# Layernorm, window attention and a gated feed-forward block: three independent reorderings of a scheduled kernel (first projections and fetch, late weight casts, a chain of weight scales)

## The chip, the cores and the metric

One core of one Trainium2 chip runs the whole kernel. The metric is device time in microseconds of one execution, the median over runs. The engines are TensorE (PE, with its weight loads as PEld), VectorE (DVE), ScalarE (ACT), GpSimd (POOL) and SyncE (SP), which issues the DMAs.

## What is computed

```
xn = layernorm(x)                                  # x: 2048 x 512
q, k, v = split(xn @ wqkv)                         # 32 heads of 16
p  = softmax(q k^T / 4, causal, window of 256)
s  = (p v) @ wo                                    # 2048 x 512
h  = silu(xn @ w1) * (xn @ w3)                     # 2048 x 1792
out = x + s * silu(h @ w2)
```

Inputs and output are float32; the products are taken in halves of f16 (a high and a low part, three products for each), so that float32 accuracy is kept.

## The kernel before

**Tiles.** The 2048 tokens go in four tiles of 512, the 32 heads in four groups of eight, the 1792 hidden units in 14 blocks of 128 (w13 for a block of w1 and w3, w2 for the way back). Within a tile the kernel projects q, k (`project`) and v (`value`), sends q and k through DRAM (`dQ`, `dK`) to bring them back in the layout of the scores (`fetch`, tiles qa and KA), finds row maxima in a first pass over the scores (`pass1`, L665 on PE and L679 on DVE), and takes the scores again, masks them (L753 on DVE), exponentiates (L756 on ACT) and multiplies by v (L774 on PE). Gate and up products (L1036, with the silu at L1051 on ACT, L1055 and L1060 on DVE), and the product with w2 (L1261) fill PE between attention steps.

**Weights.** In the first tile each weight block is loaded, its squares summed (L249 and L923 on ACT, `squares`), the sums cast (`sb`, L261 or L927 on DVE), summed over partitions on PE by a product with ones (L280 or L285), and turned into a power of two by a few one-column instructions on DVE (`powers`, L291 to L304). The block is then scaled and cut in two f16 parts: by `split` (L333 on ACT, L334 on DVE), or by `split_pool` (scale L342 and high part L343 on ACT, low part L345 on POOL). For w13, `measure` does this; for w2, `measure_down`, whose chain L935 to L945 joins the w2 norms with the power of the blocks before.

**Order.** PE runs in the order that the code gives. For the other engines a scheduler places the instructions by priority and data, within bounds set by hand: `later(n, f)` calls f n steps ahead, a step being one call of the main list; `besides` and `beside_scores` run a read beside the next bank of scores; `tc.issue_after(x)` forbids an instruction to be placed ahead of x on its engine; `lasts["emptied"]` is the last instruction that emptied a PSUM bank, and `lasts["exp"]` the last exponential (`behind_exp`). `high_priority` sections (`urgent`) come first.

**PSUM.** There are two banks m (`bank`), two banks of scores s (`scores_bank`) and the banks po. A bank is filled by PE and read by DVE or ACT; PE waits when the bank that comes next isn't read. A projection's bank is emptied by L614 (ACT, high part) and L618 (DVE, low part), one of gate and up by L1051 and L1055 or L1060.

**Start.** While the first weights arrive PE runs idle products with ones (`keep_busy`, L1537) to stay busy; behind them the transposes of the first tokens (L493), then the first projections `k00` and `q00`.

Of the kernel before, what the change touches and what calls it, by code (L numbers as in the profile page):

```python
# [10 lines left out]
F32 = mybir.dt.float32  # L11
# [10 lines left out]
P = 128  # L22
S = 2048
D = 512
F = 1792
H = 32
DH = 16
# [56 lines left out]
def tile_block(ctx: ExitStack, tc: tile.TileContext, x, wqkv, wo, w1, w3, w2, out):  # L84
# [155 lines left out]
    def squares(parts, on_act=0, apart=0):  # L240


        ssq = small.tile([P, len(parts)], F32, name="ssq")

        def one(i, raw):

            sq = ppool.tile([P, D], BF16, name="sqa" if i < on_act else "junk", bufs=1)
            if i < on_act:
                nc.scalar.activation(sq, raw, AF.Square, accum_out=ssq[:, i:i + 1])  # L249
            else:  # L250
                nc.vector.tensor_tensor_reduce(out=sq, in0=raw, in1=raw, scale=1.0, scalar=0.0,
                                               op0=ALU.mult, op1=ALU.add, accum_out=ssq[:, i:i + 1])
        for i, raw in enumerate(parts):
            if apart:
                later(apart * (i + 1), lambda i=i, raw=raw: one(i, raw))
            else:
                one(i, raw)
        sb = small.tile([P, len(parts)], BF16, name="sb")

        def cast():  # L260
            lasts["cast"] = nc.vector.tensor_copy(sb, ssq)  # L261
        def behind_bank():

            with tc.issue_after(lasts["emptied"].ins) if "emptied" in lasts else nullcontext():
                cast()
        if apart:
            later(apart * (len(parts) + 1) + 1, behind_bank)
        else:
            cast()
        return sb  # L270
# [310 lines left out]
    def project(t, g, k, terms=(range(3),), scores_bank=False):  # L581


        cell = {}

        parts = ([[(c, i) for c in (2 * half, 2 * half + 1) for i in range(3)] for half in range(2)] if len(terms) == 1
                 else [[(c, i) for i in group for c in range(NC)] for group in terms])

        def part(n):
            assert turned[t] == 4  # L590
            w = WQ[t, g, k]
            xh, xl = X[t]
            if n == 0:
                cell["pp"] = pss.tile([P, 2, TW], F32, name="s")[:, 0, :] if scores_bank else bank([P, TW])
            for c, i in parts[n]:
                a, b = ((0, xh), (1, xh), (0, xl))[i]
                nc.tensor.matmul(cell["pp"], w[:, (a * NC + c) * P:(a * NC + c + 1) * P], b[:, c, :], start=(c, i) == parts[0][0],  # L597
                                 stop=(c, i) == parts[-1][-1])
            if n < len(parts) - 1:
                return  # L600
            if t == 0:
                def store():
                    with behind_load():
                        nc.sync.dma_start(dWQ[g, k], w)
                    give(w, after=8)
                later(45, store)
            else:
                give(w)
            pp = cell["pp"]
            both = take(F16)  # L610
            B = both.rearrange("p (a t) -> p a t", a=2)
            s = QS / (XS * WS)
            with urgent():
                nc.scalar.activation(B[:, 0, :], pp, AF.Copy, scale=s)  # L614

            def rest():
                with urgent():
                    lasts["emptied"] = nc.vector.scalar_tensor_tensor(B[:, 1, :], pp, s, B[:, 0, :], op0=ALU.mult, op1=ALU.subtract)  # L618
                d = (dQ, dK)[k][g][:, :, t * TW:(t + 1) * TW]
                if k == 0:  # L620
                    nc.sync.dma_start(d[:, 0:2, :], B[:, 0:1, :].to_broadcast([P, 2, TW]))
                    nc.sync.dma_start(d[:, 2, :], B[:, 1, :])
                else:
                    nc.sync.dma_start(d[:, 0:2, :], B)
                    nc.sync.dma_start(d[:, 2, :], B[:, 0, :])
                give(both, after=4)
            later(1, rest)
        return opening([(len(l), lambda n=n: part(n)) for n, l in enumerate(parts)])
# [2 lines left out]
        WQ[t, g, k] = w = take(F16)  # L631
        nc.sync.dma_start(w, dWQ[g, k])

    def fetch(t, g):
        QA[t, g] = qa = qpool.tile([P, 4, TW], F16, name="qa")
        ka = keys(t, g)
        c0 = 0 if t else 2 * P
        for dst, d in ((ka[:, :, c0:], dK[g][:, :, t * TW - 2 * P + c0:(t + 1) * TW]),
                       (qa, dQ[g][:, :, t * TW:(t + 1) * TW])):
            for r in range(2):  # L640
                lasts["load"] = nc.sync.dma_start(dst[64 * r:64 * r + KR],
                                  d[64 * r:64 * r + 64].rearrange("(a d) i t -> (d i) a t", d=DH))

# [224 lines left out]

    measured = set()

    def measure(f, apart=0):

        raws = [RAW.pop(f + i) for i in range(2)]
        sb = squares([raws[0][0], raws[1][0], raws[0][1], raws[1][1]], on_act=4 if f > 2 else 2, apart=apart)
# [7 lines left out]
        def rest(pp, pi):  # L884
# [5 lines left out]
            def cut(i, k):  # L890
                if k == 0:
                    WF[0, f + i] = [[None, None], WF.pop((0, f + i), [None, None])[1]]
                WF[0, f + i][0][k] = a = take(F16)
                split_pool(a[:, 0:D], a[:, D:], raws[i][k], pi[:, k, i:i + 1])
                give(raws[i][k], after=5)
            for i in range(2):
                for k in range(2):
                    later(((1, 2, 4, 6) if f < 8 else (1, 5, 9, 13))[2 * i + k], lambda i=i, k=k: cut(i, k))
        if started:
            beside_scores(8, scale)  # L900
        else:
            later(10 if apart else 6, scale)

# [11 lines left out]
    def measure_down(k, f):  # L915
# [12 lines left out]

        def scale(s):
            p2 = small.tile([P, n], F32, name="pp2")  # L930
            return then(s, powers(sb, n, p2, None, s), lambda: rest(p2))

        def rest(p2):
            assert measured >= set(range(f0, f1))
# [12 lines left out]
            def cut(f):  # L947
# [3 lines left out]
                    with tc.issue_after(lasts["emptied"].ins):  # L951
                        split(b[:, 0:D], b[:, D:], raw, sw[:, f - f0:f - f0 + 1])
                else:
                    split_pool(b[:, 0:D], b[:, D:], raw, sw[:, f - f0:f - f0 + 1])
                give(raw, after=5)
            for i, f in enumerate(range(f0, f1)):
                later(1 + 2 * i, lambda f=f: cut(f))
# [335 lines left out]
    def total(t, b):  # L1293
# [4 lines left out]
        def part(half):  # L1298
# [16 lines left out]
            if half:  # L1315
# [10 lines left out]
                if t == NT - 1:  # L1326
                    store()
                else:
                    later(4, store)
                if b == 3:  # L1330
                    give(*(OT[t, g] for g in range(NG)))
        return opening([(6, lambda h=h: part(h)) for h in range(2)])
# [22 lines left out]
    def feed_forward():  # L1355
# [4 lines left out]
        for t in range(NT):  # L1360
            for f in range(FB):
                if t == 0:
# [3 lines left out]
                    elif f + LEAD == FB - 1:  # L1366
                        pieces += [(0, lambda f=f: load(0, f)) for f in range(FB - 2, FB)]
                    if f % 2 and f + 3 < FB:
                        pieces.append((0, lambda f=f + 3: later(5, lambda: measure(f, 1)) if f == 6 else measure(f, 1)))
                    pieces += [(0, lambda f=f: load_down(0, f)) for f in range(f + 2 if f else 0, min(f + 3, FB))]  # L1370
                    for m in range(f + 1 if f else 0, min(f + 2, FB)):
                        k = next(k for k, (_, f1) in enumerate(GROUPS) if m < f1)
# [158 lines left out]
        nc.gpsimd.memset(KA[2][:, a, :].bitcast(F32), TWO_ONES)  # L1531


    def keep_busy(n):
        ps = bank([P, 4, P])
        for _ in range(n):
            nc.tensor.matmul(ps, onesb, onesb.unsqueeze(1).to_broadcast([P, 4, P]), start=True, stop=True)  # L1537

# [19 lines left out]
        flush()  # L1558
    with tc.issue_after(lasts["hi"].ins), tc.issue_after(lasts["x"].ins):
        qk[1][1]()  # L1560
    keep_busy(4)


    k00, q00 = (project(0, 0, k, ((0,), (1,), (2,)), k) for k in (1, 0))
    run([k00[0], q00[0], k00[1]])
    qk[1][2]()
    with tc.issue_after(lasts["scale"].ins):
# [2 lines left out]
    qk[1][3]()  # L1570
    with tc.issue_after(lasts["hi"].ins):
        run([k00[2], q00[2]])
    later(1, lambda: fetch(0, 0))
    k01 = project(0, 1, 1, ((0, 2), (1,)))
    run(k01[:1])
    wv[2]()
# [4 lines left out]
    sc["o"] = scaled(SQ["wv"][3], OS / WS, "so")  # L1581
    with tc.issue_after(lasts["hi"].ins):
        measure(0)
    run(project(0, 1, 0, scores_bank=True))
    later(1, lambda: fetch(0, 1))
    run(value(0, True))
    qk[2][1]()
# [89 lines left out]
```

## Time and profile before

| | |
|---|---|
| median of 3 runs | 811.51 us (811.10 to 811.94) |
| the profiled execution, whole | 811.24 us |
| its span | 809.4 us |
| granted PE clock | 1.0 |
| PE busy | 793.7 us, 98% |
| DVE busy | 631.2 us, 78% |
| ACT busy | 392.1 us, 48% |
| POOL busy | 377.1 us, 47% |
| DMA moved | 134.19 MB, mean 166 GB/s |

A row of a timeline has the start in microseconds, the duration (of xN instructions of one form together), engine, line, operation and tiles, and in brackets the engine's idle time ahead of it with the instruction that ended it. A row of the table of waits has the sum, the number of times, and the longest.

### The profile page before, as it was taken

How to read it: one execution, taken by the hardware profiler on the slowest of the kernel's cores; microseconds unless marked ns; L12 is line 12 of the kernel's file. 1: busy time of each engine (PE TensorE's matmuls, PEld its weight loads, DVE VectorE, ACT ScalarE, POOL GpSimd, SP SyncE). 2: the span in 40 equal slices, each digit the busy share in tenths (PEclk: the TensorE clock that was granted, in tenths of full speed). 3: DMA queues.
4: the chain of work that ended last, by engine and by line, in shares of the span. 5: the costliest groups of instructions: out<-in, count | busy, mean ns of one | idle time of the engine just before them, and what ended most of it. 6: DMA issues, size and time to landing. Idle time of an engine off the chain costs nothing.

```text
span 809.4 us, 23944 instructions
## 1 busy us (share of the span) xinstructions
PE 793.7 (98%) x9176; PEld 403.7 (50%) x9176; DVE 631.2 (78%) x2037; ACT 392.1 (48%) x591; POOL 377.1 (47%) x732
## 2 busy tenths in 40 slices
PE   8999989999999999999999999999999999999998
PEld 4444444444444444444444454456544754466465
DVE  8788788887888777887988888777778787875437
ACT  6879586553546544345344433344444234344411
POOL 2345376342329445354353455530346276550670
PEclk9999999999999999999999999999999999999999
DMA  9968554835576474757655634646372644335321
GB/s 282 265 214 267 160 183 134 278 114 191 160 199 208 134 232 139 218 142 263 160 162 181 194 104 119 185 137 179 105 201 74 160 139 137 113 90 172 111 65 62
DMA packets 109795, 134.19 MB, mean 166 GB/s; under 512 B 18864, under 2 KB 64880, under 8 KB 109680
## 3 DMA queue, kind: packets, MB, share of 16 engines
q1 hardware_dynamic: 109392, 132.13, 54.6%
q8 instruction: 72, 1.18, 0.6%
q10 hardware_dynamic: 288, 0.52, 0.2%
q14 instruction: 43, 0.35, 0.1%
HBM read 91.23 MB, written 36.57 MB: 158 GB/s over the span
## 4 chain that ended last, share of the span: by engine, by line
PE 79%; DVE 8%; ACT 6%; DMA 3%; issue 2%; SPq 1%; POOL 0%; ACTq 0%; DVEq 0%
PE m L1036 30%; PE po L774 8%; PE m L1261 8%; PE m L1179 8%; PE m L597 7%; PE s L746 5%; PE m L1313 4%; PE m L567 4%; PE s L665 3%; DMA slot<-in_B_w_dram 2%; DVE junk L679 2%; PE po L665 2%; ACT slot L342 1%; ACT pt L756 1%; ACT sqa L249 1%
## 5 line engine op out<-in xcount | busy, mean ns | idle before, releaser
L1036 PE MATMUL m<-XH,slot 128*128 128x512 f16 x896 | 267.4, 380 | 1.6 <-DVE slot L618 1.2
L756 ACT ACTIVATE pt<-s,es 128x1024 f32<-128x1024 f32 x152 | 167.5, 1112 | 193.7 <-DVE s L753 186.5
L1036 PEld LDWEIGHTS <-slot 128*128 128x128 f16 x1344 | 124.7, 98 | 156.0 <-issue 12.0
L1036 PE MATMUL m<-XL,slot 128*128 128x512 f16 x448 | 169.9, 379 | 0.0
L753 DVE TENSOR_TENSOR s<-s,MK 128x256 f32<-128x256 f32 (+2 forms) x280 | 118.7, 434 | 51.2 <-PE s L746 47.0
L679 DVE CUSTOM_DVE_ANT_0 junk<-s,MW 128x320 bf16<-128x320 f32 x276 | 133.9, 485 | 17.9 <-PE s L665 10.3
L339 POOL TENSOR_TENSOR slot<-slot,slot 128x256 f16<-128x256 f32 (+1 forms) x86 | 57.7, 692 | 141.9 <-ACT slot L1069 76.7
L345 POOL TENSOR_TENSOR slot<-slot,slot 128x128 f16<-128x128 f32 x168 | 69.1, 446 | 58.3 <-ACT slot L343 58.3
L679 DVE CUSTOM_DVE_ANT_0 junk<-po,MW 128x320 bf16<-128x320 f32 x172 | 83.4, 485 | 4.7 <-DVE mt L704 0.3
L1261 PE MATMUL m<-slot,slot 128*128 128x512 f16 x336 | 78.6, 380 | 0.3 <-DVE slot L1055 0.3
L774 PE MATMUL po<-pt,V 64*32 64x320 f32 (+4 forms) x2880 | 77.2, 342 | 0.8 <-DVE pp L304 0.8
L597 PE MATMUL m<-XH,slot 128*128 128x512 f16 x240 | 71.0, 380 | 1.6 <-DVE slot L1055 1.2
L1179 PE MATMUL m<-slot,slot 128*128 128x256 f16 x588 | 68.4, 273 | 0.0
L1094 POOL TENSOR_TENSOR slot<-slot,slot 128x256 f16<-128x256 f32 x98 | 64.6, 671 | 1.1
L1051 ACT ACTIVATE slot<-m,sgs 128x512 f32<-128x512 f32 x56 | 38.3, 683 | 54.4 <-PE m L1036 52.3
L774 PEld LDWEIGHTS po<-pt,V 64*32 64x32 f32 x2880 | 50.5, 106 | 22.9 <-PE s L515 0.9
L1179 PEld LDWEIGHTS <-slot 128*128 128x128 f16 x588 | 56.1, 98 | 11.5 <-issue 3.0
L1055 DVE SCALAR_TENSOR_TENSOR slot<-slot,m 128x512 f32<-128x512 f32 x56 | 38.3, 684 | 29.0 <-ACT slot L1051 29.0
L746 PE MATMUL s<-qa,KA 50*64 50x320 f16 (+3 forms) x1472 | 58.4, 260 | 0.1
L597 PEld LDWEIGHTS <-slot 128*128 128x128 f16 x384 | 35.6, 98 | 44.8 <-issue 3.4
L746 PEld LDWEIGHTS <-KA 50*64 50x64 f16 x1472 | 30.1, 106 | 51.9 <-issue 30.9
L1261 PEld LDWEIGHTS <-slot 128*128 128x128 f16 x336 | 30.7, 98 | 38.6 <-issue 4.2
(189 smaller groups left out, 1138.5 us busy)
## 6 DMA issues: line engine op xcount, KB each, us to landing
slot<-dW SPq DMA_DIRECT2D x98, 256.0 KB
slot<-in_B_w_dram SPq DMA_DIRECT2D x56, 256.0 KB
slot<-dFold SPq DMA_DIRECT2D x48, 256.0 KB
dW<-slot SPq DMA_DIRECT2D x42, 256.0 KB
slot<-in_A_x_dram SPq DMA_DIRECT2D x30, 256.0 KB
KA<-dK SPq DMA_DIRECT2D x24, 288.0 KB
qa<-dQ SPq DMA_DIRECT2D x32, 192.0 KB
slot<-dWQ SPq DMA_DIRECT2D x24, 256.0 KB
```

Source lines behind the costliest of these rows:

```text
L339: op(out[:, c], a[:, c], b[:, c])
L345: nc.gpsimd.tensor_sub(lo[:, c:c + P], raw[:, c:c + P], hi[:, c:c + P])
L597: nc.tensor.matmul(cell["pp"], w[:, (a * NC + c) * P:(a * NC + c + 1) * P], b[:, c, :], start=(c, i) == parts[0][0], stop=(c, i) == parts[ ...
L679: lasts["maximum"] = nc.vector.tensor_tensor_reduce(out=junk[:, :n], in0=s[:, r, :n], in1=mask, scale=1.0, scalar=NEG, op0=ALU.add, op1=AL ...
L746: nc.tensor.matmul(s[64 * h:64 * h + 64, r, o:o + 64 * n], ka[rows, 2 * p + a, 64 * (m + 4):64 * (m + 5)], qa[rows, 2 * p + a, 64 * (m + k ...
L753: nc.vector.tensor_add(v, v, MK[:, kind, of:of + n, :].unsqueeze(1).to_broadcast([P, 2 * len(which), n, 64]))
L756: lasts["exp"] = nc.scalar.activation(pt, s, AF.Exp, scale=es)
L774: nc.tensor.matmul(cell["po"][32 * i:32 * i + 32, h, 64 * (m + k):64 * (m + k + n)], V[64 * h:64 * h + 64, (4 * t + m // 2) % VB, hd * VW: ...
L1036: nc.tensor.matmul(cell[k], w[:, (a * NC + c) * P:(a * NC + c + 1) * P], b[:, c, :], start=c == 0 and i == 0, stop=c == NC - 1 and i == 2)
L1094: nc.gpsimd.tensor_sub(lo, view, hi)
L1179: nc.tensor.matmul(cell["ps"][:, c], made[:, f:f + P], wj[:, g:g + 256], start=j == j0 and c == 0 and n == 0, stop=j == j1 - 1 and n == 2, ...
L1261: nc.tensor.matmul(ps, hh[:, a * TW + b * P:a * TW + (b + 1) * P], w[:, c * D:(c + 1) * D], start=f == f0 and i == 0, stop=f == f1 - 1 and ...
```

## The change

Line numbers of the changed kernel are higher from L641 on: by 2 up to L887 (L679, L753 and L756 become L681, L755 and L758), by 8 at L913 to L923, by 11 at L935 to L945, and by 12 further down (L1051, L1055 and L1069 become L1063, L1067 and L1081).

What it does:

- `keep_busy` ahead of the first projection makes three products instead of four, into a bank of scores in place of an m bank, and the first projection (k00) accumulates in that same bank.
- The first `fetch` brings q and k back in two parts of two heads each (eight DMAs in place of four); on SP the second store of dK moves ahead of the first of dQ, and a weight load (L395) behind the first fetch.
- The casts of w13 blocks 8 and up and of the second and later groups of w2 are bound behind the last exponential. The measurement of w13 blocks 6 and 7 starts three steps later, and its reads sit beside other scores.
- The second half of w2's scale chain is called one step later and bound behind the last emptied bank.
- The stores of the output of the first tiles come ten steps later instead of four. The cast of squares for parts two steps apart comes a step earlier.

```diff
...
             with tc.issue_after(lasts["emptied"].ins) if "emptied" in lasts else nullcontext():
...
         if apart:
-            later(apart * (len(parts) + 1) + 1, behind_bank)
+            later(apart * len(parts) + 2, behind_bank)
         else:
...
         return sb
...
             w = WQ[t, g, k]
...
             if n == 0:
-                cell["pp"] = pss.tile([P, 2, TW], F32, name="s")[:, 0, :] if scores_bank else bank([P, TW])
+                cell["pp"] = bank([P, TW]) if scores_bank is False else scores_bank()[:, 0, :]
             for c, i in parts[n]:
...
                 nc.tensor.matmul(cell["pp"], w[:, (a * NC + c) * P:(a * NC + c + 1) * P], b[:, c, :], start=(c, i) == parts[0][0],
...
         WQ[t, g, k] = w = take(F16)
...
-    def fetch(t, g):
+    def fetch(t, g, ps=None):
         QA[t, g] = qa = qpool.tile([P, 4, TW], F16, name="qa")
...
         c0 = 0 if t else 2 * P
-        for dst, d in ((ka[:, :, c0:], dK[g][:, :, t * TW - 2 * P + c0:(t + 1) * TW]),
-                       (qa, dQ[g][:, :, t * TW:(t + 1) * TW])):
-            for r in range(2):
-                lasts["load"] = nc.sync.dma_start(dst[64 * r:64 * r + KR],
-                                  d[64 * r:64 * r + 64].rearrange("(a d) i t -> (d i) a t", d=DH))
+        for heads in (slice(0, 4),) if ps is None else [slice(2 * p, 2 * p + 2) for p in ps]:
+            for dst, d in ((ka[:, heads, c0:], dK[g][:, :, t * TW - 2 * P + c0:(t + 1) * TW]),
+                           (qa[:, heads, :], dQ[g][:, :, t * TW:(t + 1) * TW])):
+                for r in range(2):
+                    rows = slice(64 * r + DH * heads.start, 64 * r + DH * heads.stop)
+                    lasts["load"] = nc.sync.dma_start(dst[64 * r:64 * r + KR],
+                                      d[rows].rearrange("(a d) i t -> (d i) a t", d=DH))
...
-    def measure(f, apart=0):
+    def measure(f, apart=0, until=8):
...
         sb = squares([raws[0][0], raws[1][0], raws[0][1], raws[1][1]], on_act=4 if f > 2 else 2, apart=apart)
...
                 WF[0, f + i][0][k] = a = take(F16)
...
                 give(raws[i][k], after=5)
+            def tied(i, k):
+                with behind_exp():
+                    cut(i, k)
             for i in range(2):
                 for k in range(2):
-                    later(((1, 2, 4, 6) if f < 8 else (1, 5, 9, 13))[2 * i + k], lambda i=i, k=k: cut(i, k))
+                    if f < 8:
+                        later((1, 2, 4, 6)[2 * i + k], lambda i=i, k=k: cut(i, k))
+                    else:
+                        later((1, 5, 9, 13)[2 * i + k], lambda i=i, k=k: tied(i, k))
         if started:
-            beside_scores(8, scale)
+            beside_scores(until, scale)
         else:
...
             p2 = small.tile([P, n], F32, name="pp2")
-            return then(s, powers(sb, n, p2, None, s), lambda: rest(p2))
+            def bound():
+                with tc.issue_after(lasts["emptied"].ins):
+                    rest(p2)
+            return then(s, powers(sb, n, p2, None, s), lambda: later(1, bound))
...
             assert measured >= set(range(f0, f1))
...
                     with tc.issue_after(lasts["emptied"].ins):
...
                 else:
-                    split_pool(b[:, 0:D], b[:, D:], raw, sw[:, f - f0:f - f0 + 1])
+                    with behind_exp():
+                        split_pool(b[:, 0:D], b[:, D:], raw, sw[:, f - f0:f - f0 + 1])
                 give(raw, after=5)
...
                 later(1 + 2 * i, lambda f=f: cut(f))
...
                 if t == NT - 1:
...
                 else:
-                    later(4, store)
+                    later(10, store)
                 if b == 3:
...
         return opening([(6, lambda h=h: part(h)) for h in range(2)])
...
                     elif f + LEAD == FB - 1:
...
                     if f % 2 and f + 3 < FB:
-                        pieces.append((0, lambda f=f + 3: later(5, lambda: measure(f, 1)) if f == 6 else measure(f, 1)))
+                        pieces.append((0, lambda f=f + 3: later(8, lambda: measure(f, 1, 6)) if f == 6 else measure(f, 1)))
                     pieces += [(0, lambda f=f: load_down(0, f)) for f in range(f + 2 if f else 0, min(f + 3, FB))]
...
                         k = next(k for k, (_, f1) in enumerate(GROUPS) if m < f1)
...
         nc.gpsimd.memset(KA[2][:, a, :].bitcast(F32), TWO_ONES)
...
-    def keep_busy(n):
-        ps = bank([P, 4, P])
+    def keep_busy(n, ps=None):
+        ps = bank([P, 4, P]) if ps is None else ps
         for _ in range(n):
...
         flush()
...
         qk[1][1]()
-    keep_busy(4)
-
-
-    k00, q00 = (project(0, 0, k, ((0,), (1,), (2,)), k) for k in (1, 0))
+    waiting = scores_bank()
+    keep_busy(3, waiting[:, 0, :].rearrange("p (k q) -> p k q", q=P))
+
+
+    k00, q00 = (project(0, 0, k, ((0,), (1,), (2,)), (lambda: waiting) if k else False) for k in (1, 0))
     run([k00[0], q00[0], k00[1]])
...
     with tc.issue_after(lasts["scale"].ins):
...
     qk[1][3]()
...
         run([k00[2], q00[2]])
-    later(1, lambda: fetch(0, 0))
+    later(1, lambda: fetch(0, 0, (0, 1)))
     k01 = project(0, 1, 1, ((0, 2), (1,)))
...
     wv[2]()
...
     sc["o"] = scaled(SQ["wv"][3], OS / WS, "so")
...
         measure(0)
-    run(project(0, 1, 0, scores_bank=True))
+    run(project(0, 1, 0, scores_bank=scores_bank))
     later(1, lambda: fetch(0, 1))
...
     qk[2][1]()
```

On ACT, when the k projection of the second head group empties its banks (L614), with L249, L923 as squares of weights and L342, L343 the scale and the high cast of w13 blocks, before:

```order
L342 ACTIVATE slot_210<-slot_210,pi 128x512
L249 ACTIVATE sqa,ssq<-slot_704 128x512
L343 CAST slot_833<-slot_210 128x512
L923 ACTIVATE sqa,ssq_737<-slot_712 128x512
L614 ACTIVATE slot_906<-m_884 128x512
L249 ACTIVATE sqa,ssq<-slot_701 128x512
L342 ACTIVATE slot_213<-slot_213,pi 128x512
L249 ACTIVATE sqa,ssq<-slot_705 128x512
L343 CAST slot_891<-slot_213 128x512
L342 ACTIVATE slot_214<-slot_214,pi 128x512
L614 ACTIVATE slot_972<-m_911 128x512
L343 CAST slot_918<-slot_214 128x512
```

and now:

```order
L249 ACTIVATE sqa,ssq<-slot_702 128x512
L342 ACTIVATE slot_210<-slot_210,pi 128x512
L249 ACTIVATE sqa,ssq<-slot_706 128x512
L614 ACTIVATE slot_908<-m_886 128x512
L343 CAST slot_835<-slot_210 128x512
L931 ACTIVATE sqa,ssq_739<-slot_714 128x512
L342 ACTIVATE slot_213<-slot_213,pi 128x512
L249 ACTIVATE sqa,ssq<-slot_703 128x512
L343 CAST slot_893<-slot_213 128x512
L614 ACTIVATE slot_974<-m_913 128x512
L249 ACTIVATE sqa,ssq<-slot_707 128x512
L342 ACTIVATE slot_214<-slot_214,pi 128x512
```

The first L614 has gone ahead of the L343 and the L923 (now L931) that stood in front of it, and the second has two rows fewer ahead of it in the program.

On ACT, around the exponentials of the second head group, at some 113 to 120 us of the profile before (es is the scale of the exponential, sw that of w2's blocks, pi that of w13's), before:

```order
L1069 CAST slot_1913<-slot_1827 128x512
L756 ACTIVATE pt<-s,es_402 128x1024
L923 ACTIVATE sqa,ssq_1992<-slot_1743 128x512
L1051 ACTIVATE slot_2001<-m_1983,sgs 128x512
L342 ACTIVATE slot_1006<-slot_1006,sw_1924 128x512
L342 ACTIVATE slot_1104<-slot_1104,sw_1924 128x512
L343 CAST slot_1974<-slot_1006 128x512
L343 CAST slot_2003<-slot_1104 128x512
L249 ACTIVATE sqa,ssq<-slot_1564 128x512
L756 ACTIVATE pt<-s,es_402 128x1024
```

and now:

```order
L758 ACTIVATE pt<-s,es_400 128x1024
L342 ACTIVATE slot_1099<-slot_1099,pi 128x512
L931 ACTIVATE sqa,ssq_1987<-slot_1745 128x512
L1063 ACTIVATE slot_2003<-m_1978,sgs 128x512
L343 CAST slot_1955<-slot_1099 128x512
L342 ACTIVATE slot_1008<-slot_1008,sw_1974 128x512
L249 ACTIVATE sqa,ssq<-slot_1566 128x512
L343 CAST slot_1990<-slot_1008 128x512
L758 ACTIVATE pt<-s,es_400 128x1024
L249 ACTIVATE sqa,ssq<-slot_1570 128x512
L342 ACTIVATE slot_1106<-slot_1106,sw_1974 128x512
L342 ACTIVATE slot_1102<-slot_1102,pi 128x512
```

Between the L1051 (now L1063) and the exponential behind it stood two L342, two L343 and one L249; now a cast of a w13 block, and one each of L342, L249 and L343. The other casts follow behind that exponential.

On DVE, w2's chain of the second group (L935 to L945) and the instruction that empties the bank behind it (L1055), before:

```order
L304 TENSOR_SCALAR pp_1851<-al 128x4
L477 TENSOR_SCALAR slot_1522<-slot_1522,mv,rs 128x512
L935 TENSOR_TENSOR pp_1851<-pp_1851,p_156 128x4
L937 TENSOR_REDUCE q<-pp_1851 128x1
L938 TENSOR_SCALAR dsc<-q 128x1
L940 TENSOR_TENSOR fq<-fq,q 128x1
L943 RECIPROCAL q<-q 128x1
L945 TENSOR_SCALAR sw_1924<-p_156,q 128x4
L1055 SCALAR_TENSOR_TENSOR slot_2001<-slot_2001,m_1983 128x512
L753 TENSOR_TENSOR s<-s,MK 128x4x64
```

and now:

```order
L304 TENSOR_SCALAR pp_1853<-al 128x4
L477 TENSOR_SCALAR slot_1524<-slot_1524,mv,rs 128x512
L946 TENSOR_TENSOR pp_1853<-pp_1853,p_156 128x4
L948 TENSOR_REDUCE q<-pp_1853 128x1
L949 TENSOR_SCALAR dsc<-q 128x1
L951 TENSOR_TENSOR fq<-fq,q 128x1
L954 RECIPROCAL q<-q 128x1
L956 TENSOR_SCALAR sw_1974<-p_156,q 128x4
L1067 SCALAR_TENSOR_TENSOR slot_2003<-slot_2003,m_1978 128x512
L755 TENSOR_TENSOR s<-s,MK 128x4x64
```

The order is the same: the chain stands where it stood, ahead of the emptying instruction (now L1067). Elsewhere on DVE single L261 casts move: that at 37.47 us of the profile before, from ahead of row maxima (L679) and of the scales (L298 to L304) of other projection weights to behind L1055 and the maxima that follow it.

## The prediction

> **What bounds the kernel now.** The busy times on the page come first, then the table by stage, then what TensorE (PE) waited for.
>
> ```profile
> PE 793.7 (98%) x9176; PEld 403.7 (50%) x9176; DVE 631.2 (78%) x2037; ACT 392.1 (48%) x591; POOL 377.1 (47%) x732
> ...
> 0.00:180.00 180.00, 168.95 (x1622) 79.33 (x1623) 148.14 (x558) 130.22 (x245) 84.12 (x213) 1.00 0.70 212
> 180.00:750.00 570.00, 569.54 (x7021) 291.63 (x7020) 449.47 (x1418) 247.52 (x324) 263.24 (x468) 1.00 0.54 160
> ```
>
> After the span, each stage's columns are PE, PEld, DVE, ACT, POOL busy time, granted clock, DMA share and GB/s. From 180 to 750 us PE is idle for 0.46 of 570 us: nothing on another engine can gain there, and the change takes one small matmul from PE and adds none. In the first 180 us PE is idle for 11.05 us. Those are the stake. The edits act there, and what PE gains there the full stretch behind passes on to the end.
>
> ```profile
> PE s L665 <- ACT pt L756: 2.4, 2, 1.6
> PE m L1036 <- DVE slot L618: 1.2, 2, 1.0
> PE m L597 <- DVE slot L1055: 1.2, 1, 1.2
> ...
> PE po L665 <- DVE M L679: 0.8, 1, 0.8
> PE po L774 <- DVE pp L304: 0.8, 1, 0.8
> ...
> PE m L1537 <- DVE XL L501: 0.6, 1, 0.6
> ...
> PE s L665 <- DMA qa<-dQ: 0.4, 1, 0.4
> ```
>
> Each row gives the sum, the times and the longest. All but the fetch of qa are one pattern: a PSUM bank that ACT or DVE empties too late, since that engine had other work in front. So for each edit I ask which row stands in front of the emptying instruction, and by how much it moves.
>
> **The change part by part.** *Keep-busy.* The four idle-filling matmuls took an m bank and so waited 0.58 us for its reader; now three go into a scores bank, where the first projection then accumulates.
>
> ```profile
> 12.85 1.02 PE L1537 MATMUL m<-onesb 128*128 128x512 bf16 x4 [0.58 <-DVE XL L501]
> 13.71 1.03 PE L597 MATMUL s<-XH,slot 128*128 128x512 f16 x4
> ...
> 12.41 0.62 ACT L496 CAST XH<-s 128x512 f16<-128x512 f32 x1
> ...
> 15.67 0.16 DVE L261 CAST sb<-ssq 128x2 bf16<-128x2 f32 x1
> ...
> 16.30 0.19 PE L280 MATMUL s<-sb,onesb 128*128 128x1 bf16 x2
> ```
>
> The projection can start when XH's last cast ends (13.03) instead of at 13.71: 0.6 us. But the L280 behind it would then come at 15.7 and waits until sb is cast (15.83), so 0.45 us is left. Bounds 0 to 0.65.
>
> *The first fetch.* dK's second store goes ahead of dQ's first, a 256 KB weight load moves behind the fetches, and each fetch is cut in head pairs, the first of which suffices for the waiting matmul.
>
> ```profile
> 25.39 0.88 SPq L641 DMA_DIRECT2D qa<-dQ x2
> ...
> 30.15 0.30 PE L665 MATMUL s<-KA,qa 48*64 48x128 f16 x7 [0.41 <-DMA qa<-dQ]
> ```
>
> The second of these qa issues ends at 26.27 and PE goes on at 30.15: 3.9 us from issue to use. A fetch is four transfers of 48 x 4 x 512 f16, 768 KB; now 384 KB suffice, and the 256 KB load is behind them. At the 212 GB/s of the first 180 us the 640 KB less are about 3 us; PE, 0.45 us ahead, needs 0.9 of them. The wait of 0.41 goes. Bounds 0 (the halves take as long as wholes) to 0.65 (the broken rhythm beside the idle time).
>
> *The cast of sb for the next weights.* On DVE it stood ahead of the maxima and the scale chain of the weights before, and waited there; now it stands behind L1055.
>
> ```profile
> 37.47 0.17 DVE L261 CAST sb<-ssq 128x2 bf16<-128x2 f32 x1 [1.60 <-ACT sqa L249]
> ...
> 41.87 0.38 PE L1036 MATMUL m<-XL,slot 128*128 128x512 f16 x1
> 42.29 0.59 PE L1036 MATMUL m<-XH,slot 128*128 128x512 f16 x2
> ```
>
> The 1.6 us that DVE waited here come off everything behind it: the scales (L302), the two L333 on ACT, L1051 and L1055. At PE, L1055 was late by little: 0.42 us between starts instead of 0.22. Gain 0.2, bounds 0 to 0.3; the larger part shows at the next place.
>
> ```profile
> 53.02 0.72 ACT L342 ACTIVATE slot<-slot,pi 128x512 f32<-128x512 f32 x1
> 53.65 0.58 ACT L614 ACTIVATE slot<-m 128x512 f16<-128x512 f32 x1
> ...
> 55.33 0.59 PE L1036 MATMUL m<-XH,slot 128*128 128x512 f16 x2 [1.03 <-DVE slot L618]
> ```
>
> ACT works through casts without a break up to this L614. Ahead of the L614 before it stood an L343 and an L923 which now stand behind, and all of them start earlier by up to the 1.6 us that DVE no longer waits. So this L614, and the L618 that follows it on DVE, come some 1.6 us earlier, more than the 1.03 that PE waits. The 1.03 us go. Bounds 0.3 (ACT or the bank's filling holds L614 at about 53) to 1.2 (with the broken rhythm).
>
> *Casts tied behind exponentials.* Scale (L342) and hi cast (L343) of late w13 and w2 blocks now alternate with the exponentials L756.
>
> ```profile
> 115.25 0.28 DVE L679 CUSTOM_DVE_ANT_0 junk<-s,M 128x128 bf16<-128x128 f32 x1
> 115.45 0.29 DVE L753 TENSOR_TENSOR s<-s,MK 128x128 f32<-128x128 f32 x1
> ...
> 115.68 1.12 ACT L343 CAST slot<-slot 128x512 f16<-128x512 f32 x2
> ...
> 117.33 1.09 ACT L756 ACTIVATE pt<-s,es 128x1024 f32<-128x1024 f32 x1
> ...
> 118.47 0.30 PE L665 MATMUL s<-KA,qa 48*64 48x256 f16 x4 [1.62 <-ACT pt L756]
> ```
>
> The scores were masked by 115.74; the exponential came 1.6 us later, behind two L342, two L343 and an L249. It now has one of each in front. An L342 is worth 0.63 (53.02 to the next start at 53.65), an L343 0.56 (half of 1.12): 1.2 us earlier, 116.15, with the mask done by then. But two of the deferred L342 come to stand ahead of a later L1051, whose bank ends the next wait:
>
> ```profile
> 125.18 0.67 ACT L1051 ACTIVATE slot<-m,sgs 128x512 f32<-128x512 f32 x1
> ...
> 130.37 0.94 PE L774 MATMUL po<-pt,V 64*32 64x320 f32 x24 [0.82 <-DVE pp L304]
> ```
>
> That L1051 moves up by only about 0.7, so the second wait grows by 0.45. Net 0.75; bounds -0.3 (the later wait takes more than the gain) to 1.6.
>
> ```profile
> 165.05 0.29 DVE L753 TENSOR_TENSOR s<-s,MK 128x128 f32<-128x128 f32 x1
> ...
> 166.02 1.11 ACT L756 ACTIVATE pt<-s,es 128x1024 f32<-128x1024 f32 x1
> ...
> 167.18 0.30 PE L665 MATMUL s<-KA,qa 48*64 48x256 f16 x4 [0.73 <-ACT pt L756]
> ```
>
> Here the mask is done at 165.34 and the exponential starts 0.7 later. Between L614 and it stood two L343 and two L342; now two L343 and an L923. One pass of 0.63 less, with some 0.1 for the read behind L923: 0.5 us. Bounds 0 to 0.73.
>
> *The chain of w2's scales.* The words say that it comes a step later, but on DVE its six instructions, L935 to L945, stand in all four groups in the same place, ahead of L1055:
>
> ```profile
> 113.68 0.72 DVE L945 TENSOR_SCALAR sw<-p,q 128x4 f32<-128x4 f32 x1
> 114.32 0.68 DVE L1055 SCALAR_TENSOR_TENSOR slot<-slot,m 128x512 f32<-128x512 f32 x1
> ...
> 115.04 0.59 PE L597 MATMUL m<-XH,slot 128*128 128x512 f16 x2 [1.19 <-DVE slot L1055]
> ```
>
> PE's 1.19 us behind them stay. I count zero; bounds 0 to 0.5 (L945 was slow here, and may be quicker).
>
> *The rest.* Out stores go ten steps late instead of four, POOL's L339 pairs move ahead of some L345: PE waited for no store and for no POOL row, so zero; what it costs when this cover is gone is rival D.
>
> Sum: 0.45 + 0.41 + 0.2 + 1.03 + 0.75 + 0.5 = 3.3 us. The profiled execution took 811.24; less 3.3 it is 807.9. The median of the runs is 0.27 above it: 808.2.
>
> **The rivals.** *B, taken back by ACT.* Before 60 us the sum has 2.1 us. Behind it comes the stage in which ACT has least room:
>
> ```profile
> 60.00:80.00 20.00, 18.70 (x147) 8.24 (x146) 17.10 (x64) 18.92 (x37) 10.86 (x22) 1.00 0.83 267
> ```
>
> ACT is busy for 18.92 of 20 us, and PE waits there for 1.3 us in all. If ACT's work comes no earlier (its weights come by DMA, at a share of 0.83), PE arrives 2.1 us sooner and waits 2.1 longer. Left are 0.75 + 0.5: 811.51 - 1.25 = 810.3. Against it: the delays taken away before 60 us lay on DVE and ACT themselves. Chance 0.16.
>
> *C, the fetch is no sooner.* Eight transfers instead of four: if each half takes as long as a whole, the 0.41 stay, and 808.6 follows. [...] Chance 0.1.
>
> *D, slower: tied casts come late.*
>
> ```profile
> ACT pt L756 <- DVE s L753: 186.5, 106, 8.0
> ...
> 123.97 1.58 POOL L345 TENSOR_TENSOR slot<-slot,slot 128x128 f16<-128x128 f32 x4 [0.91 <-ACT slot L343]
> ...
> 132.35 1.47 PE L1261 MATMUL m<-slot,slot 128*128 128x512 f16 x6
> ```
>
> ACT waits 1.76 us on average for a mask ahead of an exponential. A cast that used to fill this wait now stands behind it. The last w2 block was ready on POOL at 125.55 and used at 132.35: 6.8 us, of which PE's earlier arrival takes 2.8 and an L1051 (0.67) and an L343 (0.56) put in front 1.2. If more than the 2.8 left fall on that chain, PE waits: four waits of 1.76 are 7.0, 4.2 of them stall, and 808.2 + 4.2 = 812.4; if other groups fare likewise, more. Against it: those casts' matmuls lie well behind. Chance 0.18.
>
> *E, the chain is quicker after all.* If L1055 is reached without L935 to L945 the 1.19 us go too: 807.0. The unmoved rows speak against it. Chance 0.08.
>
> **How the numbers follow.** The forecast, 808.2, has 0.48. Its own bounds: at best 0.65 + 0.65 + 0.3 + 1.2 + 1.6 + 0.73 + 0.5 = 5.6 (805.9), at worst 0 (811.5, all lower ends together). The range goes from 805.5 to 812.8, with D's upper half and a little below E left out. A measurement can tell about 0.2%, 1.6 us: faster means below 809.9. Forecast, C and E give faster 0.64 with a little of B, 0.66; the rest of B and of the forecast's low end give same 0.15; D and mishaps give slower 0.19.
>
> **What would show it.** In the profile after: no wait of L665 for qa at 30; no L618 wait at 54; DVE's L261 gap of 1.6 us at 37 gone; the exponential at 117.3 right behind one L343, and PE's wait there below 0.7; the wait for L1055 at 115 still near 1.2; waits at 73 to 77 no longer than 1.5 in sum. Wrong would be a wait of PE for a POOL or ACT slot at L1261 or L1036, or idle time of PE above 11 us in the first 180.

## The result

The changed kernel takes 808.44 us (median of 5 runs, 808.19 to 808.65) against 811.26 us: a ratio of 0.9964, 95% interval 0.9953 to 0.9974. The forecast was 808.2 in a range of 805.5 to 812.8. In the profiled execution the span went from 809.4 to 806.4 us.

The page of the changed kernel (busy time of each engine), and its table by stage, with the bounds of the last stages shifted by 3 us:

```profile
PE 792.3 (98%) x9175; PEld 403.6 (50%) x9175; DVE 630.9 (78%) x2037; ACT 392.5 (49%) x591; POOL 377.5 (47%) x732
```

```profile
0.00:180.00 180.00, 170.87 (x1653) 80.50 (x1653) 150.45 (x570) 131.49 (x246) 84.24 (x215) 1.00 0.70 210
180.00:747.00 567.00, 566.48 (x7004) 290.39 (x6991) 447.04 (x1405) 246.99 (x323) 263.42 (x467) 1.00 0.55 160
```

PE idles for 9.13 us in the first 180 us where it idled for 11.05, and has got through more work by then; behind that it is as full as before. Of the 3.0 us between the two spans 0.17 is a first load that came earlier in this execution (L280 starts at 8.72 instead of 8.89). What PE waited for in the changed kernel (sum, times, longest):

```profile
PE po L776 <- DVE pp L304: 1.5, 1, 1.5
...
PE s L280 <- DVE sb L261: 1.0, 1, 1.0
PE s L667 <- ACT pt L758: 0.9, 2, 0.7
...
PE m L1048 <- DVE slot L618: 0.8, 2, 0.6
PE m L597 <- DVE slot L1067: 0.7, 1, 0.7
```

The wait for qa is gone, those for the exponential (2.4), for L618 (1.2) and for the bank behind w2's chain (1.2) are smaller, and one, for a po bank, has grown from 0.8 to 1.5. The wait of L280 has grown too, from 0.4 to 1.0, but costs nothing: the idle products ahead of it took 6.66 us in this execution instead of 7.46, and L280 itself does not come later. PE's rows at these places:

```profile
12.91 1.02 PE L597 MATMUL s<-XH,slot 128*128 128x512 f16 x4 [0.17 <-ACT XH L496]
...
28.93 0.60 PE L667 MATMUL s<-KA,qa 48*64 48x128 f16 x8
...
53.46 0.59 PE L1048 MATMUL m<-XH,slot 128*128 128x512 f16 x2 [0.63 <-DVE slot L618]
...
112.60 0.59 PE L597 MATMUL m<-XH,slot 128*128 128x512 f16 x2 [0.73 <-DVE slot L1067]
...
115.14 0.30 PE L667 MATMUL s<-KA,qa 48*64 48x256 f16 x4 [0.74 <-ACT pt L758]
...
127.70 0.70 PE L776 MATMUL po<-pt,V 64*32 64x320 f32 x9 [1.49 <-DVE pp L304]
...
163.92 0.30 PE L667 MATMUL s<-KA,qa 48*64 48x256 f16 x4 [0.15 <-ACT pt L758]
```

Against before: 0.8 us earlier at the first projection, no wait for qa, 1.03 to 0.63, 1.19 to 0.73, 1.62 to 0.74, 0.82 to 1.49, 0.73 to 0.15.

### The profile page after: what moved, and what is told of

Read it like the earlier page. It is cut to its first block, busy times and chain, and to the rows that moved or that the text cites. A ratio compares the mean times of both kernels' runs of the same rounds, so it can differ in the third digit from the quotient of the medians.

```text
span 806.4 us, 23975 instructions
## 1 busy us (share of the span) xinstructions
PE 792.3 (98%) x9175; PEld 403.6 (50%) x9175; DVE 630.9 (78%) x2037; ACT 392.5 (49%) x591; POOL 377.5 (47%) x732
## 4 chain that ended last, share of the span: by engine, by line
PE 83%; DVE 6%; ACT 6%; DMA 2%; issue 2%; SPq 1%; POOL 0%; DVEq 0%; ACTq 0%
PE m L1048 30%; PE po L776 9%; PE m L1273 9%; PE m L597 8%; PE m L1191 8%; PE s L748 5%; PE m L1325 4%; PE m L567 4%; PE s L667 3%; PE po L667 2%; ACT pt L758 1%; DVE junk L681 1%; ACT slot L342 1%; DMA slot<-in_B_w_dram 1%; ACT slot L343 1%
## 5 line engine op out<-in xcount | busy, mean ns | idle before, releaser
L758 ACT ACTIVATE pt<-s,es 128x1024 f32<-128x1024 f32 x152 | 167.6, 1113 | 190.9 <-DVE s L755 179.2
L755 DVE TENSOR_TENSOR s<-s,MK 128x256 f32<-128x256 f32 (+2 forms) x280 | 118.8, 435 | 51.9 <-PE s L748 48.9
L681 DVE CUSTOM_DVE_ANT_0 junk<-s,MW 128x320 bf16<-128x320 f32 x276 | 134.1, 486 | 17.6 <-PE s L667 9.8
L339 POOL TENSOR_TENSOR slot<-slot,slot 128x256 f16<-128x256 f32 (+1 forms) x86 | 57.6, 692 | 126.8 <-ACT slot L1081 56.7
L345 POOL TENSOR_TENSOR slot<-slot,slot 128x128 f16<-128x128 f32 x168 | 68.8, 445 | 69.7 <-ACT slot L343 67.7
L681 DVE CUSTOM_DVE_ANT_0 junk<-po,MW 128x320 bf16<-128x320 f32 x172 | 83.5, 485 | 4.7 <-DVE al L298 0.4
L1273 PE MATMUL m<-slot,slot 128*128 128x512 f16 x336 | 78.6, 380 | 0.1
L1063 ACT ACTIVATE slot<-m,sgs 128x512 f32<-128x512 f32 x56 | 38.3, 683 | 54.0 <-PE m L1048 53.8
L1067 DVE SCALAR_TENSOR_TENSOR slot<-slot,m 128x512 f32<-128x512 f32 x56 | 38.3, 685 | 28.6 <-ACT slot L1063 27.1
L1273 PEld LDWEIGHTS <-slot 128*128 128x128 f16 x336 | 30.7, 98 | 38.4 <-issue 4.0
```

The lines of the kernel that those rows point to most:

```text
L339: op(out[:, c], a[:, c], b[:, c])
L345: nc.gpsimd.tensor_sub(lo[:, c:c + P], raw[:, c:c + P], hi[:, c:c + P])
L681: lasts["maximum"] = nc.vector.tensor_tensor_reduce(out=junk[:, :n], in0=s[:, r, :n], in1=mask, scale=1.0, scalar=NEG, op0=ALU.add, op1=AL ...
L755: nc.vector.tensor_add(v, v, MK[:, kind, of:of + n, :].unsqueeze(1).to_broadcast([P, 2 * len(which), n, 64]))
L758: lasts["exp"] = nc.scalar.activation(pt, s, AF.Exp, scale=es)
L1273: nc.tensor.matmul(ps, hh[:, a * TW + b * P:a * TW + (b + 1) * P], w[:, c * D:(c + 1) * D], start=f == f0 and i == 0, stop=f == f1 - 1 and ...
```

## The experiments

**Which edit earns.** Four kernels split the change. e1 has the edits of `keep_busy`, `project` and `fetch` alone:

```diff
-    keep_busy(4)
+    waiting = scores_bank()
+    keep_busy(3, waiting[:, 0, :].rearrange("p (k q) -> p k q", q=P))
...
-    later(1, lambda: fetch(0, 0))
+    later(1, lambda: fetch(0, 0, (0, 1)))
```

> Only the new start (three idle products in a scores bank, k00 in that bank) and the first fetch in head pairs. Theory A (each edit earns at its own place): the waits at 12, 30, 42 and 54 us shrink, about 1.9 us in all, as in the changed kernel up to 80 us; the waits at 113 (1.19) and 116 (1.63) stay as they were: about 809.4. Rival B (what is won at the start is taken back by ACT before 120 us, and the tied casts earn the rest): 810.5 or more, with longer waits at 113 to 130.

e2 has the two `behind_exp` of `tied` and of w2's `split_pool` alone:

```diff
+                    with behind_exp():
+                        split_pool(b[:, 0:D], b[:, D:], raw, sw[:, f - f0:f - f0 + 1])
```

> Only the late w13 and w2 casts bound behind the exponentials. Theory A: PE's waits at 113.5 go from 1.19 to about 0.7, since POOL has less to do beside DVE's chain, at 116.6 from 1.63 to 0.7, at 166 from 0.73 to 0.15, and the one at 129 grows from 0.82 to 1.5: 1.3 us less, about 810.0. Rival C (the headline edit carries these gains): all four waits as before, 811.3.

e3 has the edit of w2's scale chain alone (the expectations call it the headline edit), and e4 all but it:

```diff
-            return then(s, powers(sb, n, p2, None, s), lambda: rest(p2))
+            return then(s, powers(sb, n, p2, None, s), lambda: later(1, bound))
```

> Only the second half of w2's scale chain called a step later and behind the last emptied bank. Theory A: DVE's order is the same, on ACT the second L342 of w2 changes places with passes of squares and the exponential at 117 comes some 0.3 later: 811.3, 0.3 more at most, with the wait for L1055 at 113.5 still about 1.2. Rival C (the headline edit earns): the waits at 113 and 116 shrink by over 1 us together, 810 or less.

> All edits but the one on w2's scale chain. Theory A: as the changed kernel, 808.4, within 0.3; the exponential at 114 has an L342 ahead of it in place of an L249, about the same length. Rival C: a microsecond or more above it, 809.5.

| kernel | median, us | ratio to before (95%) |
|---|---|---|
| e1, start and fetch alone | 810.90 | 0.9994 (0.9984 to 1.0003) |
| e2, ties alone | 810.75 | 0.9992 (0.9983 to 1.0001) |
| e3, chain edit alone | 811.40 | 1.0000 (0.9991 to 1.0010) |
| e4, all but the chain edit | 808.62 | 0.9966 (0.9953 to 0.9979) |

The edit of the chain is worth nothing that these runs can tell, by itself and on top of the rest. In the table of waits of e3 stands what stood before:

```profile
PE s L665 <- ACT pt L756: 2.5, 2, 1.7
...
PE m L597 <- DVE slot L1058: 1.2, 1, 1.2
```

The ties do at their places what was expected of them. PE's rows in e2:

```profile
114.65 0.59 PE L597 MATMUL m<-XH,slot 128*128 128x512 f16 x2 [0.73 <-DVE slot L1062]
117.20 0.30 PE L665 MATMUL s<-KA,qa 48*64 48x256 f16 x4 [0.74 <-ACT pt L756]
...
129.78 0.51 PE L774 MATMUL po<-pt,V 64*32 64x320 f32 x8 [1.50 <-DVE pp L304]
```

But e2 missed its 810.0 by 0.75 us: by the start times of the same products its PE is 0.9 us ahead of the kernel before at 167 us, and loses 0.3 at 237 and 0.3 at 717 again. At 237 it waits 0.35 us for a cast of squares (L261).

e1 and e2 together make up 1.1 us of the 2.8. e1 missed its 809.4 by 1.5 us: where did that go? Up to 80 us e1 runs as the changed kernel does, and at 115 its PE is still 1.8 us ahead of the kernel before; at 338 it is 1.0 ahead, and from 516 on 0.75 (why it loses again at 516 stays open). Its PE and SP rows at 334 us show a wait that neither of the two kernels had:

```profile
333.57 0.34 SPq L1326 DMA_DIRECT2D out_dram<-slot  x1
333.95 0.43 SPq L632 DMA_DIRECT2D slot<-dWQ  x1
...
337.11 0.60 PE L597 MATMUL m<-XH,slot 128*128 128x512 f16 x2 [0.61 <-DMA slot<-dWQ]
```

In e1 an out store holds SP until POOL has added the residual (the store goes at 333.57), and the load of a projection weight queues behind it (333.95). Before, POOL began that sum at 331.14; e1's POOL does one more pair of L1009 and a pair of L339 ahead of it (rows of POOL in e1; `x4` holds this pair and the sum's, which ends at 333.55, and the store goes at 333.57):

```profile
329.60 1.31 POOL L1009 TENSOR_TENSOR slot<-slot,slot 128x256 f16<-128x256 f32 x2 [0.17 <-ACT slot L1005]
330.87 2.68 POOL L339 TENSOR_TENSOR slot<-slot,slot 128x256 f16<-128x256 f32 x4
```

PE, ahead by what it won, gets there before the load does. In the changed kernel the store is called ten steps late, and the load stands ahead of it:

```profile
324.21 0.49 SPq L632 DMA_DIRECT2D slot<-dWQ  x1
...
332.01 0.34 SPq L1336 DMA_DIRECT2D out_dram<-slot  x1
```

**The late stores.** Two kernels test this: the change without its edit of the stores, and e1 with it.

```diff
-                    later(10, store)
+                    later(4, store)
```

> The changed kernel with the out stores four steps late again instead of ten. Theory D (the late stores are what lets the gain of the first 180 us through): on SP the load of a projection weight (L632) stands again behind an out store that waits for POOL until 332; it is issued at 332.4 and lands some 3.1 us later, as in e1, at 335.5, where PE wants it at 334.8: a wait of about 0.7 for L632 that the changed kernel hasn't, 809.1. Rival E (the stores are beside the path): no such wait, 808.4.

> The new start and fetch of e1, and the out stores ten steps late. Theory D: e1's wait of 0.61 at 336 for the load L632 is gone, and what was won at the start reaches the end: about 810.2, or 0.7 below e1. Rival E: as e1, 810.9.

e5 takes 809.39 us (0.9976, 0.9966 to 0.9986), 0.95 above the changed kernel, and the wait is back:

```profile
332.02 0.34 SPq L1336 DMA_DIRECT2D out_dram<-slot  x1
332.40 0.43 SPq L632 DMA_DIRECT2D slot<-dWQ  x1
...
335.41 0.61 PE L597 MATMUL m<-XH,slot 128*128 128x512 f16 x2 [0.45 <-DMA slot<-dWQ]
```

e6 takes 810.16 us (0.9986, 0.9976 to 0.9995), 0.74 below e1, and on SP the load goes at 327.22, the store at 334.23. Theory D holds in both directions. The wait itself is 0.45 to 0.61 us. By start times e5's PE, level with the changed kernel's at 235 us, is 0.64 behind at this product (335.41 against 334.77), and 0.27 more at 715, where it waits 0.25 for L1067; whether the second loss follows from the first was not tested.

The start, the ties and the late stores account for 1.8 us of the 2.8 (0.63 in e2, 1.17 in e6). One edit that none of e1, e2 and e6 has shows in their profiles: the cast of squares that is bound a step earlier. e6's PE, like e2's, waits for it at 237 us, for 0.49; in the changed kernel it ends at 231.05, over 3 us before PE's L285 at 234.27. No kernel was run with this edit alone, so that it makes up the rest is not shown.

**The chain and POOL.** Why did the wait at 113 shrink, when DVE's order there did not change? First POOL's row in the kernel before, then DVE's rows in the changed kernel, with POOL's:

```profile
109.83 3.92 POOL L345 TENSOR_TENSOR slot<-slot,slot 128x128 f16<-128x128 f32 x9
```

```profile
110.14 0.16 DVE L304 TENSOR_SCALAR pp<-al 128x4 f32<-128x4 f32 x1
110.21 0.53 DVE L477 TENSOR_SCALAR slot<-slot,mv,rs 128x512 f32<-128x512 f32 x1
...
111.50 0.23 DVE L956 TENSOR_SCALAR sw<-p,q 128x4 f32<-128x4 f32 x1
111.86 0.69 DVE L1067 SCALAR_TENSOR_TENSOR slot<-slot,m 128x512 f32<-128x512 f32 x1
...
108.64 1.30 POOL L339 TENSOR_TENSOR slot<-slot,slot 128x256 f16<-128x256 f32 x2 [1.91 <-ACT slot L1081]
112.41 1.58 POOL L345 TENSOR_TENSOR slot<-slot,slot 128x128 f16<-128x128 f32 x4 [2.47 <-ACT slot L343]
```

POOL worked beside the whole chain before; now it is idle from 109.94 to 112.41, and the last instruction of the chain took 0.23 us instead of 0.72. e9 puts POOL to work there and changes no order elsewhere:

```diff
-                    halves(nc.gpsimd.tensor_sub, hh[:, TW:], sg, hh[:, 0:TW])
+                    for _ in range(3 if (t, f) == (0, 6) else 1):
+                        halves(nc.gpsimd.tensor_sub, hh[:, TW:], sg, hh[:, 0:TW])
```

> The changed kernel with one L339 pair of POOL, ahead of w2's second chain, done three times over with the same result, so that POOL is busy until about 112.5 instead of 109.9; the order on all other engines is the same. Theory H (POOL's work beside them makes DVE's small instructions slow, and this is why the changed kernel's wait at 113 was shorter): L298 to L956 take 3.4 us again instead of 2.8, L956 0.4 or more instead of 0.23, PE's wait for L1067 goes from 0.73 to about 1.2: 808.9. Rival J (the order and the data alone set the chain): 2.8 us, 0.73, 808.4.

It takes 809.48 us, 1.04 more than the changed kernel. POOL's row, DVE's and PE's:

```profile
108.73 4.17 POOL L339 TENSOR_TENSOR slot<-slot,slot 128x256 f16<-128x256 f32 x6 [1.92 <-ACT slot L1081]
...
110.23 0.63 DVE L304 TENSOR_SCALAR pp<-al 128x4 f32<-128x4 f32 x1
110.78 0.97 DVE L477 TENSOR_SCALAR slot<-slot,mv,rs 128x512 f32<-128x512 f32 x1
...
113.15 0.23 DVE L956 TENSOR_SCALAR sw<-p,q 128x4 f32<-128x4 f32 x1
...
114.03 0.59 PE L597 MATMUL m<-XH,slot 128*128 128x512 f16 x2 [2.07 <-DVE slot L1067]
```

L304, four columns wide, goes from 0.16 to 0.63, L477 from 0.53 to 0.97, and L956, behind POOL's end at 112.9, is quick again. From L298 to L956 it is 4.35 us (109.03 to 113.38) instead of 2.79, more than the 3.4 expected. Theory H holds, and its size was set too low. L304 and L477 grow by 0.47 and 0.44 us, less than one of POOL's six L339 takes (4.17 us together, 0.70 each). By what means POOL's work slows them, no row shows.

**The chain moved in truth.** e7 calls it five steps later, and there it does stand behind L1067 on DVE.

```diff
-            return then(s, powers(sb, n, p2, None, s), lambda: later(1, bound))
+            return then(s, powers(sb, n, p2, None, s), lambda: later(5, bound) if k == 1 else later(1, bound))
```

> The changed kernel with w2's second chain (L946 to L956) called five steps later, so that on DVE it stands behind the instruction that empties the bank (L1067), which the change's words say. Theory F (with POOL off, the chain ends at 111.73 and L1063 on ACT at 111.82, so ACT is the bound by now): PE's wait at 113 goes from 0.73 to 0.65 only; the exponential at 114 comes up to 0.4 earlier, with an L342 and an L343 fewer and one more L249 ahead: about 808.1. Rival G (the chain in front still is the bound): the wait goes to 0.1 or less, 807.7 or below.

It takes 807.43 us (0.9953, 0.9939 to 0.9968), 1.0 below the changed kernel, yet not where rival G had it. DVE's and ACT's rows:

```profile
111.99 0.69 DVE L1067 SCALAR_TENSOR_TENSOR slot<-slot,m 128x512 f32<-128x512 f32 x1 [1.11 <-ACT slot L1063]
...
111.28 0.68 ACT L1063 ACTIVATE slot<-m,sgs 128x512 f32<-128x512 f32 x1
```

and its table of what PE waits for:

```profile
PE po L776 <- DVE XL L525: 0.7, 1, 0.7
PE m L597 <- DVE slot L1067: 0.7, 1, 0.7
...
PE s L667 <- ACT pt L758: 0.5, 2, 0.4
```

With the chain out of the way DVE idles 1.11 us for L1063, and PE's wait there is 0.73 as in the changed kernel: theory F, though its total, 808.1, was 0.7 too high. The gain stands in two later waits: for the exponential (0.9 to 0.5) and for the po bank (1.5 to 0.7). That ACT's casts behind the chain bring it fits the order that was expected, but was not tested by itself.

**Eight casts on POOL.** e8 moves high casts of the changed kernel, those of w2's second group and of w13 blocks 8 and 9:

```diff
-        nc.scalar.copy(hi, raw)
+        if on_pool:
+            halves(lambda o, x, _: nc.gpsimd.tensor_copy(o, x), hi, raw, raw)
+        else:
+            nc.scalar.copy(hi, raw)
```

> The changed kernel with eight high casts (w2's second group and w13 blocks 8 and 9) on POOL in two halves each instead of as L343 on ACT. If ACT's passes set the waits at 113, 114 and 126 (0.73, 0.74, 1.49), these shrink by up to 1.5 us in all: 807. If POOL's work beside DVE's chain and small instructions sets them, the wait at 113 goes back to 1.1 or more and the total to 808.5 or above.

It takes 812.68 us (1.0016, 1.0001 to 1.0031). Neither reading foresaw what happened: the wait at 113 stayed at 0.72, and the loss is at another place:

```profile
121.25 6.32 DVE L827 TENSOR_SCALAR dr<-dr,so 128x32 f32<-128x32 f32 x1
...
125.97 1.57 POOL L348 TENSOR_TENSOR slot<-slot,slot 128x128 f16<-128x128 f32 x4
...
128.56 1.46 PE L1276 MATMUL m<-slot,slot 128*128 128x512 f16 x3 [4.29 <-DVE slot L1070]
```

An instruction of 32 columns took 6.32 us, until POOL's row of casts and subtractions ended at 127.54; the L1070 behind it kept PE waiting for 4.29. The wait is not the whole loss: the profiled execution took 813.58 us against 808.19 of the changed kernel, 5.39 more. PE was slower behind the wait: three L1276 took 1.46 us, as long as six of them in the changed kernel (L1273, at 129.68 us, 1.47). The granted PE clock of this execution was 0.995 in the mean, where the changed kernel's was 1.0. The nine runs of e8 spread from 810.97 to 815.99, with the lower mean clocks in the longer ones: 0.995 to 0.996 in the three above 813, 0.999 or 1.0 in the four up to 811.3.

**What holds L618 at 53 us.** In e10, made from e7, `rest` of one projection is called at once. (The two L614 that the section on the change shows are those of the k and q projections of the third head group, not of the k projection of the second.)

```diff
-            later(1, rest)
+            rest() if (t, g, k) == (0, 2, 0) else later(1, rest)
```

> The kernel of e7 with the L618 of the q projection of the third head group called at once and not a step later, so that on DVE it goes ahead of two row maxima and three small instructions at 52 us. Theory K (DVE's own queue holds L618 there, not ACT's L614): PE's wait at 52.6 goes from 0.63 to under 0.1, and the sum to about 806.8, less what the scales behind it (L333, L334) then come late. Rival L (L614 holds it): 0.63 as before, 807.4.

In the changed kernel ACT's and DVE's rows read:

```profile
51.32 0.59 ACT L614 ACTIVATE slot<-m 128x512 f16<-128x512 f32 x1
...
52.32 0.48 DVE L681 CUSTOM_DVE_ANT_0 junk<-po,MW 128x320 bf16<-128x320 f32 x1
52.72 0.69 DVE L618 SCALAR_TENSOR_TENSOR slot<-m,slot 128x512 f16<-128x512 f32 x1
```

L614 ended at 51.91, and L618 came 0.8 later, behind row maxima. In e10 L618 goes at 52.07:

```profile
52.07 0.69 DVE L618 SCALAR_TENSOR_TENSOR slot<-m,slot 128x512 f16<-128x512 f32 x1
...
52.82 0.59 PE L1048 MATMUL m<-XH,slot 128*128 128x512 f16 x2
```

PE goes on without the wait, and e10 takes 806.65 us (0.9943, 0.9928 to 0.9958), the best of these kernels: 0.8 below e7, 1.8 below the changed kernel. The 0.78 us won here are not simply carried on: by 72 us PE has lost them (L1273 now waits 0.52 for L1067), and at 75 us a wait of 0.84 for row maxima, which e7 has, is gone.

**The fetch whole again.** e11 is the changed kernel with

```diff
-    later(1, lambda: fetch(0, 0, (0, 1)))
+    later(1, lambda: fetch(0, 0))
```

> The changed kernel with the first fetch whole again (four transfers in place of eight); the weight load stays behind it. Theory M (the bytes ahead decide): 384 KB more at some 210 GB/s, qa lands 1.8 us later than 27.9, at 29.6, and PE waits about 0.7 for it at 29: 809.1. Rival N (each half takes as long as a whole): qa lands as in the changed kernel, no wait for it, 808.4.

It takes 809.40 us. qa is waited for twice, 0.9 us in all:

```profile
30.36 0.30 PE L665 MATMUL s<-KA,qa 48*64 48x128 f16 x7 [0.59 <-DMA qa<-dQ]
```

The four issues end at 26.07, and PE can go on 4.3 us later; in the changed kernel they end at 25.85, and PE finds qa there at 28.93, without a wait. Half a fetch does not take as long as a whole one: theory M. Here the weight load is behind the fetch too, and from issue to use it is 4.3 us, no less than the 3.9 before; so what helps is the halving, and moving the load earned nothing that this run shows. DVE and ACT have some rows in another order in e11, so not all of the difference of 0.96 need be the fetch's.

## Why the prediction was right

The total was right to 0.2 us, and the mechanism too: banks emptied late because of what stood in front, and PE passing the gain on. That the sum came so close is in part luck. Two terms were 1.2 us too large together (L618 by 0.63, the first tied exponential by 0.54), gains that the prediction put at little or nothing made up for it, and the late stores, put at nothing, were needed for PE to pass on the gain.

- *Keep-busy*, 0.45 expected: L280 came at 15.72 instead of 16.30, 0.58; but the transposes ahead (L493) already started 0.16 earlier in this execution, so the edit is worth 0.42.
- *Fetch*, 0.41: the wait for qa went; by start times PE's lead grew from 0.58 to 0.90 (30.24 against 29.34 in the rows below), so 0.32. e11 refutes rival C: there the whole fetch is the later one. What eight transfers cost in bandwidth against four these runs do not show: PE waited here for the first half alone.
- *The cast of sb*, 0.2: between the qa scores and the transposed maxima PE won 0.43, more than the bound of 0.3, as these rows of before and after show (30.24 to 45.30 and 29.34 to 43.97 us, 15.06 and 14.63).

```profile
30.24 0.32 PE L665 MATMUL po<-KA,qa 48*64 48x256 f16 x4
45.30 0.22 PE L698 MATMUL s<-identh,NM 64*64 64x64 f16 x2
```

```profile
29.34 0.30 PE L667 MATMUL po<-KA,qa 48*64 48x256 f16 x4
43.97 0.19 PE L700 MATMUL s<-identh,NM 64*64 64x64 f16 x2
```

- *L614 and L618 at 53*, 1.03: only 0.40. The step that failed is that L618 comes as much earlier as L614 does. L618 stood behind DVE's own maxima; e10 shows that this was the rest of the wait.
- *The first tied exponential*, 1.2 less 0.45: 0.88 less 0.67, so 0.21 instead of 0.75. The second wait was seen, but both sizes were off.
- *The exponential at 166*, 0.5: 0.58.
- *w2's chain*, 0: right for the edit (e3, e4), wrong for the place. The wait went from 1.19 to 0.73, by the tied casts, which take POOL's work away beside DVE's chain (e2 has 0.73 without the edit of the chain, and in e9, with POOL at work there, it is 2.07). The bound of 0.5 held.
- *The rest*, 0: wrong for the late stores. "PE waited for no store" was read from the kernel before; with PE ahead, SP's queue became a wait (e1), which the late stores take away (e5, e6). They are worth 0.95 us here. The earlier cast of squares at 237 us, which the prediction did not count either, is described above.

Of the signs that the prediction named, three came out otherwise: PE still waits for L618 at 53 (0.63), its wait for the exponential at 115 is 0.74 and not below 0.7, and the wait behind w2's chain is not near 1.2.

Rival B was close in kind: a gain at the start was indeed taken back in e1, yet by SP's queue at 336 us and not by ACT at 73. Rival D's POOL lateness did not come with the change. Near its place, though, at a product with w2, e8 lost 4.29 us, by DVE held up rather than by a cast that comes late. Rival E did not happen either: the chain is still in front of L1067, and the wait there shrank for another reason.

## What to carry to other kernels

Here a part of what was won before the full stretch was lost where a load stood behind a waiting store: in e1 the load was issued 0.38 us after the store and PE waited 0.61 for it, and with the stores late (e6) the kernel took 0.74 less. So look along the DMA queue for a store that waits ahead of a load, as PE will get to that load earlier. Ask of an emptying instruction what stands ahead of it on both of the engines in its chain: at 53 us PE's wait went from 1.03 to 0.63 when L614 came earlier, and the 0.63 went only when L618 did (e10). And read from the order what an edit in fact moves: the edit of w2's scale chain moved nothing on the engine that it was about, while a bigger step of it, which did, was worth 1.0 us.

## What was not expected of the hardware

Some of DVE's instructions of four columns take 0.15 to 0.23 us with POOL idle and 0.4 to 0.7 beside POOL's subtractions (L304 0.16 and 0.63, L956 0.23 and, as L945 before, 0.72). Not all do: before, L298 took 0.17 beside them, and in e9 L948 and L949, which write one column, took 0.16 and 0.15. With POOL at work without a break an instruction of 32 columns took 6.32 us (e8): it ended at 127.57, when the last of some sixteen POOL instructions had ended (127.54), while in e9 L304 and L477 grew by 0.47 and 0.44, less than the 0.70 of one L339. Why it took so long stays open; the same instruction (L824) took 0.47 in the changed kernel, with POOL busy as well (L345 from 117.51 to 122.22).
